# First units of the next batch one place earlier on TensorE, and PSUM tiles shared by the filter stage and the FFN

## The chip, the cores and the metric

The kernel runs on one core of a Trainium2 chip (trn2). The metric is the device time of one execution in microseconds; of several executions the median is taken. All arithmetic is fp32.

## The reference

Two blocks run one after the other. The first is a long convolution of each channel, done by FFT, with a filter that a small MLP makes; the second is a feed-forward network with a maximum of three products.

```python
B, S, D, FO, DFF = 4, 12544, 128, 64, 768
h = (relu(pos_emb @ w1) @ w2) * exp(-0.01 * arange(S))[:, None]   # (S, D)
u = x * v                                                         # (B, S, D)
y = irfft(rfft(u, n=2*S, axis=1) * rfft(h, n=2*S, axis=0), n=2*S)[:, :S]
t = (x * y).reshape(B * S, D)
out = maximum(maximum(t @ W1, t @ W2), t @ W3) @ W_out            # (B*S, D)
```

## The kernel before

The FFT is written as matrix products in three stages, with 90 frequencies k1 in 45 pairs (NK = 45). A batch's input is cut into 32 **units** of four columns. `u_load` brings a unit in, `u_mul` (L375) forms x*v on VectorE, a transpose (`u_turn`, L380) lays it out, and `u_products` (L418) does the first stage: 16 matmuls into one or two PSUM banks, then a copy of half of the result to SBUF on ScalarE (`high`, L440) and two additions per piece on VectorE (L444), which write the tile `spec`. A unit can be done in two halves of 8 matmuls, each with its own bank, copy and pair of additions. The `high` tiles share two buffers.

The program has four parts:

- Up to about 110 us: the filter's MLP, and the first stage of batch 0 and of the filter.
- The **filter stage** (loop at L1101, steps s = 0 to 47). Each step takes one pair of frequencies further: `s_second` and `s_filter` (L1060) make the filter's spectrum, `g_second` the second stage of batch 0, then VectorE multiplies (`g_re`, `g_im`, `g_unfold`, L577 to L589), and three steps later `g_third` (L593) does the inverse stage, whose result ScalarE copies (`zs`, L604) and SP stores in DRAM (`zd`, L605).
- The **passage** out of that loop: steps 45 to 47 have nothing left for `s_second`, and TensorE is given other work between the last three `g_third`: units 0 and 1 of batch 1 (`unit`, L1096), and the folding of the first FFN matrix into the last one. `fold(f)` (L1020) transposes a block of a weight (L1022), ScalarE copies it (`w1t`, L1024), and two matmuls add its product to the tile `pl`; `folding` issues the transpose of f and then the product of f - 1. After that come the units 2, 3 and half of 4 (L1188), the last stage of the first tile (`t_last`, L741), which needs `zd` read back (`zt`, L703) and combined on VectorE (`t_sums`, L734), and the rest of unit 4.
- The **slots**: 32 tiles per batch in six slots each. In a slot TensorE does `up` (two products of the FFN, L156 into `hps`) and `down` (one into `ops`), and beside them steps of the next batch's convolution that `conv_steps` (L608) has laid into slots by hand-written rules. For batch 1, six units are loaded before the slots (`EARLY = 6`), and unit 5's products stand in the third slot (slot number 2, L618). The last batch has no convolution beside it and a shorter form of the second FFN product (`products`).

The order on each engine is the order in which the Python code issues the instructions; an engine takes its instructions in that order, and waits by semaphores. A PSUM tile may be written again only when the readers of its last content are done.

PSUM has eight banks. In the filter stage they are three for `cps` (tag `cv`, taken in turn by `g_second`, `g_third` and `fold`), two for `sps` tag `h` (one tile, `s_filter`), one for `sps` tag `pl` (the turned units, then `pl`), and two for `gps`. The first two units get their banks from a list of their own:

```python
    def banks_of():
        for pool, tag, n in ((gps, "g", 1), (gps, "g", 1), (sps, "h", 2), (gps, "g", 1),
                             (cps, "cv", 1), (gps, "g", 1)):
            yield pool.tile([P, 512 * n], FP32, tag=tag, name="ps1")[:, 0:512]
```

In the slots they are three `hps`, two pairs `cps` (1024 wide) and one `ops`. These pools are opened after the filter stage's are closed.

Of the kernel before, what the change touches and what calls it, by code (L numbers as in the profile page):

```python
# [10 lines left out]
FP32 = mybir.dt.float32  # L11
# [4 lines left out]
PSUM = bass.MemoryType.PSUM  # L16
P = 128
# [25 lines left out]
def tables(NB):  # L43
    S = P * N1
    k1 = np.arange(N1).reshape(2, N1 // 2).T.ravel()
    n = np.arange(NB)
    a = e(np.outer(n, k1 + 0.25) / N1)
    f1 = np.concatenate([a.real, a.imag], 1)
    up = e(np.outer(n + 0.5, k1 + 0.25) / N1)
    f1q = np.stack([np.concatenate([up.real, up.imag], 1), f1], 1)  # L50
    f1h = np.zeros((64 + HH, 2, 2 * N1))
    f1h[:HH, 0], f1h[64:, 0] = f1[:HH], f1[HH:NH]
    f1h[:HH, 1], f1h[64:, 1] = f1[HH:NH], f1[:HH]
    f4 = np.stack([a.T.real, a.T.imag], 1) / S
    f4p = f4[::2].transpose(1, 0, 2).reshape(N1, NB // 2, 2).transpose(0, 2, 1)
    f4 = np.stack([up.T.real, up.T.imag], 1) / S
    f4s = f4[::2].transpose(1, 0, 2).reshape(N1, NB // 2, 2).transpose(0, 2, 1)
    f4q = np.stack([f4p, f4s * np.array([1, -1])[:, None]], 1)
    j, t = np.arange(64), np.arange(64)
    tw = (k1[:, None, None] + 0.25) / S  # L60
    half = []
    for r in range(2):
        s2 = (127 - 2 * t - r)[None, :, None]
        half.append(stacked(e(tw * s2 + j[None, None, :] * s2 / 128)))
    fwd = np.stack(half, 2)
    half = []
    for q in range(2):
        s2 = (2 * t + q)[None, None, :]
        half.append(stacked(e(-tw * s2 - j[None, :, None] * s2 / 128)))
    inv = np.stack(half, 2)  # L70
    both = np.stack([fwd, inv], 2)
    both = both.reshape(N1 // 2, 2, P, 2, 256).transpose(0, 2, 3, 1, 4)
    both = both.reshape(N1 // 2, P, 2, 512)
    j, t = np.arange(32), np.arange(32)
    quarter = [[], []]
    for v in range(2):
        for w in range(2):
            s2 = (63 - 2 * t - v)[None, :, None]
            quarter[0].append(stacked(e(tw * s2 + (2 * j + w)[None, None, :] * s2 / 128)))
            s2 = (2 * t + w)[None, None, :]  # L80
            quarter[1].append(stacked(e(-tw * s2 - (2 * j + v)[None, :, None] * s2 / 128)))
    quarter = np.stack([np.stack(q, 1) for q in quarter], 1)
    quarter = quarter.reshape(N1 // 2, 2, 2, 2, 2, 64, 64).transpose(0, 3, 5, 2, 1, 4, 6)
    quarter = quarter.reshape(N1 // 2, P, 2, 256)
    steps = np.zeros((N1 // 2 + LATE, P, 2, 256))
    steps[:N1 // 2, :, 0], steps[LATE:, :, 1] = quarter[:, :, 0], quarter[:, :, 1]
    f32 = np.float32
    return tuple(np.ascontiguousarray(t, f32) for t in (f1q, f1h, f4q, both, steps))


@with_exitstack
def kernel(
# [289 lines left out]
    def u_turn(u):  # L382
        if u % 2 == 0:
            uts[u] = uts[u + 1] = utp.tile([NB, 16, 2, 32], FP32, tag="uT", name="uT")
        ps = state["turn"]()
        turn(u, ps)
        nc.scalar.copy(uts[u][:, 8 * (u % 2):8 * (u % 2) + 8],
                       ps[0:NB, :].rearrange("n (s t r) -> n s r t", s=8, r=2))
# [62 lines left out]
    def u_first(*args):  # L451
        u_products(*args)()
# [155 lines left out]
    def conv_steps(b, done):  # L608
# [4 lines left out]
        def at(slot, late, fn, *args):  # L613
            out.append((slot, late, len(out), fn, args))

        for u in range(5, done):  # L618
            at(2 * (u - 4), 1, u_first, u)
        lead, low = (1, -NT * NF) if b > 1 else (6, 0)  # L620
        share = UNIT * (NU - done - 1)
        per_pair = (END - lead - 6) / (share + (NK + LATE) // 2 * 2 - 2)
# [147 lines left out]

    def down(i, f, h):
        if f == 0:
            pos_[i] = ops.tile([D, 512], FP32, tag="ops", name="ops")
            halves_mm(pos_[i][:, 0:N], lin[:], gs[i][:].rearrange("d p n -> d (p n)"), True,
                      False)
        halves_mm(pos_[i][:, 0:N], wo_sb[:, f, :], h[:], False, f == NF - 1)
        if f < NF - 1:
            return
        gs.pop(i)
        o = op_.tile([D, 4, NB], FP32, tag="o", name="ot")  # L780
        nc.scalar.copy(o[:].rearrange("d p n -> d (p n)"), pos_.pop(i)[:, 0:N])  # L781
        dst = outT.rearrange("d (p b n) -> d p b n", b=B, n=NB)[:, 4 * i[1]:4 * i[1] + 4, i[0], :]
        nc.gpsimd.dma_start(dst, o[:])  # L783
# [112 lines left out]
    def load_dir(g, a):  # L896
        w = lwp.tile([P, 2, 2, P], FP32, tag=f"w{a}", name="wt")
        nc.sync.dma_start(w[:].rearrange("p k r m -> p (k r m)"), wt_d[g, :, a, :])
        return w
# [100 lines left out]


    cvp = pro.enter_context(tc.tile_pool(name="cvp0", bufs=3))
    cps = pro.enter_context(tc.tile_pool(name="cps0", bufs=3, space=PSUM))
    sps = pro.enter_context(tc.tile_pool(name="sps", bufs=1, space=PSUM))
    gps = pro.enter_context(tc.tile_pool(name="gps", bufs=2, space=PSUM))
    def banks_of():
        for pool, tag, n in ((gps, "g", 1), (gps, "g", 1), (sps, "h", 2), (gps, "g", 1),
                             (cps, "cv", 1), (gps, "g", 1)):
            yield pool.tile([P, 512 * n], FP32, tag=tag, name="ps1")[:, 0:512]

    free = banks_of()

    def bank():
        return next(free)

    state = {"cv": (cvp, cps), "xb": 2, "bank": bank,
             "turn": lambda: sps.tile([P, 512], FP32, tag="pl", name="pst")}
    Gs, minus = {}, {}

    def fold(f):  # L1020
# [72 lines left out]
        if len(folded) > 1:  # L1093
            folded.pop(0)()

    def unit(u):  # L1096
        for h in range(2):
            u_first(u, 2 * h, 2)

    s_minus(0)  # L1100
    for s in range(NK + 3):  # L1101
        if s < NK:
            ws[s, 0] = wf[s]
            s_second(s)
            if s + 1 < NK:
                s_minus(s + 1)
            g_second(s)
            wf.pop(s)
            if s + 3 < NK:
                wf[s + 3] = load_dir(s + 3, 0)  # L1110
        if 1 <= s <= NK:
            g_swap(s - 1)
            s_filter(s - 1)
        if s >= 3:
            ws[s - 3, 1] = wi.pop(s - 3)
            g_third(s - 3)
            if s < NK:
                wi[s] = load_dir(s, 1)
        ready = [g for g in {NK: (s - 2, s - 1)}.get(s, (s - 2,)) if 0 <= g and s <= NK]
        for g in {NK - 2: (s - 2, s - 1), NK - 1: (s - 1,), NK: (s - 1,)}.get(s, (s - 2,)):  # L1120
            if 0 <= g and s <= NK:
                s_store(g)
        for g in ready:
            g_re(g)
            g_im(g)
            g_unfold(g)
        if s < NK:
            g_butterfly(s)

        if s in muls:  # L1130
            u_mul(muls[s])
        if s in turns:
            u_turn(turns[s])
        if s in loads:
            u_load(1, loads[s])
        if s == NK:
            unit(0)
            pl = sps.tile([P, 512], FP32, tag="pl", name="pl")
        if s == NK + 1:
            for f in range(2):  # L1140
                folding(f)
    unit(1)
    state["turn"] = bank
    for f in range(2, NF):
        folding(f)
        if f in (2, 3):
            u_turn(f + 2)
    folded.pop()()
    nc.scalar.copy(lin[:], pl[:, 0:D])
    pro.close()  # L1150
# [11 lines left out]
    wp = conv.enter_context(tc.tile_pool(name="wp", bufs=3))  # L1162
    hh = conv.enter_context(tc.tile_pool(name="hh", bufs=2))
    cvp = conv.enter_context(tc.tile_pool(name="cvp", bufs=3))
    hps = ctx.enter_context(tc.tile_pool(name="hps", bufs=1, space=PSUM))
    cps = conv.enter_context(tc.tile_pool(name="cps", bufs=1, space=PSUM))
    ops = conv.enter_context(tc.tile_pool(name="ops", bufs=1, space=PSUM))
    hbanks = itertools.cycle([hps.tile([P, 512], FP32, name=f"hps{i}") for i in range(3)])
    pairs = itertools.cycle([cps.tile([P, 1024], FP32, name=f"cps{i}") for i in range(2)])
    state = {"bank": lambda: next(pairs)}  # L1170

# [10 lines left out]
    for n, (b, i) in enumerate(tiles[:LAST]):  # L1182
        if i == 0:
            plan, pairs_from = plans[b]
        if n == 0:
            t_load(*tiles[0])
            t_load(*tiles[1])
            second_, third = u_products(2), u_products(3)  # L1188
            fourth = u_products(4, 0, 2, ops.tile([D, 512], FP32, tag="ops", name="ps1"))
            t_sums(tiles[0], nc.vector)  # L1190
            second_()
            fourth[0]()
            t_last(tiles[0], next(hbanks))
            rest = u_products(4, 2, 2, state["bank"]())
            third()
        for f in range(NF):

# [35 lines left out]
    singles = itertools.cycle([cps.tile([P, 512], FP32, name=f"last{i}") for i in range(3)])  # L1233
    state = {"bank": lambda: next(singles)}
    ops = ctx.enter_context(tc.tile_pool(name="ops2", bufs=1, space=PSUM))
    banks = [ops.tile([P, 512], FP32, name=f"ops{i}") for i in range(2)]


    tw = lp.tile([P, 3, NC, 64], FP32, name="tw", bufs=1)
# [12 lines left out]
    for i in range(0, NT, 2):  # L1252
        h = {}
# [67 lines left out]
```

## Time and profile before

| what | value |
|---|---|
| median of 3 runs | 2274.02 us (2273.86 to 2278.21) |
| the profiled execution | 2272.58 us, its span 2270.8 us |
| TensorE busy | 2254.6 us, 99% of the span |
| VectorE / ScalarE / GpSimd busy | 1562.1 / 1175.4 / 879.1 us |
| passage, 281 to 304.3 us | TensorE busy 20.20 of 23.33 us |
| slots of batches 1 to 3, 307.4 to 1850 us | TensorE busy 1541.34 of 1542.59 us |

In the profile, PE is TensorE's matmuls, PEld its weight loads, DVE VectorE, ACT ScalarE, POOL GpSimd and SP the engine that issues most DMAs. An fp32 matmul leaves two records, so that a unit's 16 matmuls show as x32. A bracket after a row gives how long the engine stood idle before it, and what ended that. Lines of the helper `halves_mm` are all L156; the tile names tell them apart (`ps<-ab,wt` is `g_third`, `pl<-wo_sb,w1t` a product of the folding, `hps<-f4p` the last stage, `hps<-gt,w_sb` the FFN).

### The profile page before, as it was taken

The numbers are of one execution on the slowest core, as the hardware profiler recorded it, in microseconds if no ns is written. First come the engines' busy times: TensorE is split into PE (matmuls) and PEld (weight loads), VectorE is DVE, ScalarE is ACT, GpSimd is POOL, SyncE is SP. The second block draws the span as 40 slices with busy tenths as digits, with TensorE's granted clock in tenths as the row PEclk, the third lists the DMA queues.
The fourth block names the chain that finished last, engine by engine and source line by source line (L and its number), as shares of the span: only waits on it lengthen the run. The fifth ranks groups of instructions, "written<-read, shape, count | busy, mean of one in ns | idle before, by whom it ended". The sixth has DMA issues, their size and how long they took to land.

```text
span 2270.8 us, 68490 instructions
## 1 busy us (share of the span) xinstructions
PE 2254.6 (99%) x27855; PEld 1376.4 (61%) x27855; DVE 1562.1 (69%) x2857; ACT 1175.4 (52%) x2130; POOL 879.1 (39%) x1089
## 2 busy tenths in 40 slices
PE   9999999999999999999999999999999999999998
PEld 8999866655555556655555556655555556666665
DVE  5589967677777667667878757667878754444443
ACT  3688844366666534456666534456666522222222
POOL 1145434223333234323333234423333326666666
PEclk9999999999999999999999999999999999999999
DMA  8788999799989589789999789879999732222221
GB/s 194 179 253 277 295 197 182 139 221 248 239 222 244 157 182 178 157 195 252 247 234 231 191 173 178 170 181 244 243 238 236 195 82 56 57 72 65 57 56 22
DMA packets 473365, 411.03 MB, mean 181 GB/s; under 512 B 327993, under 2 KB 374522, under 8 KB 473050
## 3 DMA queue, kind: packets, MB, share of 16 engines
q1 hardware_dynamic: 446034, 329.50, 64.5%
q0 software_dynamic: 26224, 75.44, 11.0%
q8 instruction: 219, 3.59, 0.7%
q10 hardware_dynamic: 792, 1.72, 0.3%
q14 instruction: 96, 0.79, 0.1%
HBM read 262.84 MB, written 84.67 MB: 153 GB/s over the span
## 4 chain that ended last, share of the span: by engine, by line
PE 98%; DVE 1%; DMA 1%; ACT 0%; issue 0%; SPq 0%; POOL 0%; POOLq 0%; DVEq 0%; ACTq 0%
PE hps L156 44%; PE ops L156 19%; PE ops L828 6%; PE cps L428 5%; PE ps L156 4%; PE cps L156 4%; PE cps L495 3%; PE ps L165 3%; PE cps L505 3%; PE sps L1060 2%; PE gps L1042 2%; PE last L156 1%; PE ps L380 1%; PE ps L342 1%; DMA wt<-wt_const 0%; DVE spec L444 0%
## 5 line engine op out<-in xcount | busy, mean ns | idle before, releaser
L156 PE MATMUL hps<-gt,w_sb 128*64 128x392 f32 x6144 | 1149.3, 494 | 0.0
L765 ACT ACTIVATE hid<-hps 128x392 f32<-128x392 f32 x768 | 383.9, 500 | 699.3 <-PE hps L156 679.5
L156 PEld LDWEIGHTS hps<-gt,w_sb 128*64 128x64 f32 x6144 | 431.3, 137 | 420.4 <-issue 384.4
L768 DVE TENSOR_TENSOR hid<-hid,hps 128x392 f32<-128x392 f32 x768 | 428.4, 558 | 331.7 <-PE hps L156 316.2
L156 PE MATMUL ops<-hid,wo_sb 128*64 128x392 f32 x2304 | 480.2, 492 | 0.0
L547 POOL TENSOR_TENSOR cb<-cb,xs 128x512 f32<-128x512 f32 x135 | 174.1, 1290 | 463.6 <-DVE xs L544 346.9
L156 PEld LDWEIGHTS ops<-hid,wo_sb 128*64 128x64 f32 x2304 | 172.3, 137 | 207.0 <-issue 199.4
L520 DVE TENSOR_TENSOR cb<-cps,eo 128x512 f32<-128x512 f32 (+1 forms) x288 | 175.2, 650 | 73.1 <-ACT eo L517 73.1
L444 DVE TENSOR_TENSOR spec<-cps,high 128x360 f32<-128x360 f32 x188 | 140.2, 786 | 118.8 <-ACT high L440 118.7
L783 POOL DMA_DIRECT2D out_dram<-ot x96 | 75.4, 785 | 346.1 <-ACT ot L781 311.6
L535 ACT ACTIVATE xs<-cb 32x512 f32<-32x512 f32 x270 | 169.5, 628 | 20.2 <-DVE cb L520 11.1
L536 ACT COPY xs<-cb 32x512 f32<-32x512 f32 x270 | 166.3, 616 | 3.2
L440 ACT COPY high<-cps 128x360 f32<-128x360 f32 (+1 forms) x94 | 74.8, 796 | 176.8 <-PE cps L428 143.5
L551 DVE TENSOR_TENSOR xs<-cb 128x256 f32<-128x256 f32 x270 | 140.9, 566 | 9.2 <-POOL cb L547 9.0
L428 PEld LDWEIGHTS cps<-f1q,uT 98*64 98x64 f32 x2992 | 129.7, 137 | 28.7 <-issue 23.1
L428 PE MATMUL cps<-f1q,uT 98*64 98x90 f32 x2992 | 134.1, 241 | 2.1 <-DVE uT L411 1.1
L396 POOL COPY planes<-ut 128x784 uint16<-128x784 uint16 x90 | 76.3, 848 | 146.5 <-DVE ut L375 138.1
L528 POOL DMA_DIRECT2D zd<-cb x135 | 92.8, 687 | 61.4 <-DVE cb L520 56.7
L156 PEld LDWEIGHTS cps<-f4p,even 90*64 90x64 f32 x1552 | 89.9, 138 | 34.8 <-issue 32.6
L852 POOL DMA_DIRECT2D out_dram<-o x128 | 77.7, 612 | 51.3 <-DVE o L845 49.1
L156 PE MATMUL cps<-f4p,zt 90*64 90x49 f32 x1552 | 96.3, 222 | 0.0
L156 PE MATMUL cps<-f4p,even 90*64 90x49 f32 x1552 | 95.0, 220 | 0.0
(147 smaller groups left out, 3154.8 us busy)
## 6 DMA issues: line engine op xcount, KB each, us to landing
ht<-hd SPq DMA_DIRECT2D x264, 256.0 KB, 6.8
wt<-wq_const SPq DMA_DIRECT2D x144, 256.0 KB, 6.5
zd<-cb POOLq DMA_DIRECT2D x135, 256.0 KB, 6.1
zt<-zd SPq DMA_DIRECT2D x384, 90.0 KB, 3.0
sq<-spec SPq DMA_DIRECT2D x264, 128.0 KB, 7.0
ut<-in_xr_dram SPq DMA_DIRECT2D x128, 196.0 KB, 3.9
ut<-in_vr_dram SPq DMA_DIRECT2D x128, 196.0 KB, 4.2
xT<-in_x_dram SPq DMA_DIRECT2D x256, 98.0 KB, 3.4
```

The source lines that it names most:

```text
L156: nc.tensor.matmul(out[64 * h:64 * h + 64], lhsT[:, 64 * h:64 * h + 64], rhs, start=start, stop=stop, skip_group_check=True)
L428: nc.tensor.matmul(ps[64 * c:64 * c + 64, 256 * i + h * N1:256 * i + (h + 1) * N1], t[:, 2 * ((at + i) % 8) + h].rearrange("n r t -> n (r ...
L444: nc.vector.tensor_tensor(out=spec[:, :, a, at:at + n], in0=v[:, 1], in1=highs[0], op=op)
L520: nc.vector.tensor_tensor(out=cb[:, a, lo:hi], in0=ps[:, lo:hi], in1=eo[:, lo:hi], op=op)
L528: nc.gpsimd.dma_start(zd[b][2 * z:2 * z + 2].rearrange("k c t a f -> (k c t) a f"), zss.pop(z))
L535: nc.scalar.mul(xs[at:at + 32], xt[at + 32:at + 64], -1.0)
L536: nc.scalar.copy(xs[at + 32:at + 64], xt[at:at + 32])
L547: nc.gpsimd.tensor_tensor(out=xts[g], in0=xts[g], in1=xs[:], op=ALU.add)
L551: nc.vector.tensor_tensor(out=ab[:, q], in0=y[:, 0], in1=y[:, 1], op=(ALU.subtract, ALU.add)[q])
L765: nc.scalar.activation(h[:], pa[:, 0:N], Relu)
L768: nc.vector.tensor_tensor(out=h[:], in0=h[:], in1=pb[:, 0:N], op=ALU.max)
L828: nc.tensor.matmul(ps[64 * c:64 * c + 64, 0:H2], w, rhs[:, H2 * c:H2 * c + H2], start=start, stop=True, skip_group_check=True)
```

## The change

The units move one place up in TensorE's order. Unit 0 (both halves, in the two `gps` banks) is issued ahead of `s_filter(44)` in step 45. Unit 1's first half comes after `g_third(42)`, its second half after the first product of the folding and ahead of `g_third(44)`. Unit 2 is done in halves within the folding. After the folding come the units 3, 4 and the first half of 5, and after the first tile's last stage the second half of 5. Nothing of `u_products` is left in the third slot. ScalarE's copies and VectorE's additions of these pieces keep the order of the units and are issued by `finish`.

PSUM: three tiles `hps` and one tile `solo` are made ahead of the filter stage and kept to the end. `Banks` hands out `hps` in turn where `cps` stood, `up` uses the same three tiles in the slots, `solo` serves the turned units, `pl`, half of unit 5, `ops`, and one of the two tiles of the last batch. Each unit names the bank that it takes: `side()` is one of the two `gps`, `bank()` the next `hps`.

```diff
+class Banks:
+    def __init__(self, tiles):
+        self.tiles = itertools.cycle(tiles)
+
+    def tile(self, shape, dtype, tag, name):
+        return next(self.tiles)
...
-        for u in range(5, done):
-            at(2 * (u - 4), 1, u_first, u)
...
-            pos_[i] = ops.tile([D, 512], FP32, tag="ops", name="ops")
+            pos_[i] = solo
...
-    cps = pro.enter_context(tc.tile_pool(name="cps0", bufs=3, space=PSUM))
+    hps = ctx.enter_context(tc.tile_pool(name="hps", bufs=1, space=PSUM))
+    hps = [hps.tile([P, 512], FP32, name=f"hps{i}") for i in range(3)]
+    solo = ctx.enter_context(tc.tile_pool(name="ops", bufs=1, space=PSUM))
+    solo = solo.tile([P, 512], FP32, name="ops")
     sps = pro.enter_context(tc.tile_pool(name="sps", bufs=1, space=PSUM))
     gps = pro.enter_context(tc.tile_pool(name="gps", bufs=2, space=PSUM))
-    def banks_of():
...
-    free = banks_of()
+    cps = Banks(hps)
 
     def bank():
-        return next(free)
+        return cps.tile([P, 512], FP32, tag="cv", name="ps1")
+
+    def side():
+        return gps.tile([P, 512], FP32, tag="g", name="ps1")
 
     state = {"cv": (cvp, cps), "xb": 2, "bank": bank,
-             "turn": lambda: sps.tile([P, 512], FP32, tag="pl", name="pst")}
+             "turn": lambda: solo}
...
-    def unit(u):
-        for h in range(2):
-            u_first(u, 2 * h, 2)
+    def finish(parts):
+        for fn in parts:
+            fn()
...
+        if s == NK:
+            unit0 = [u_products(0, 2 * h, 2, side()) for h in range(2)]
         if 1 <= s <= NK:
             g_swap(s - 1)
             s_filter(s - 1)
...
         if s == NK:
-            unit(0)
-            pl = sps.tile([P, 512], FP32, tag="pl", name="pl")
+            for part in unit0:
+                finish(part)
+            part = u_products(1, 0, 2, bank())
+            pl = solo
         if s == NK + 1:
+            finish(part)
             for f in range(2):
                 folding(f)
-    unit(1)
+            part = u_products(1, 2, 2, side())
+    finish(part)
     state["turn"] = bank
+    part = u_products(2, 0, 2, side())
+    both_ = sps.tile([P, 1024], FP32, tag="h", name="ps1")
     for f in range(2, NF):
         folding(f)
         if f in (2, 3):
             u_turn(f + 2)
+        if f == 3:
+            finish(part)
+            part = u_products(2, 2, 2, both_)
+    finish(part)
     folded.pop()()
     nc.scalar.copy(lin[:], pl[:, 0:D])
     pro.close()
...
-    hps = ctx.enter_context(tc.tile_pool(name="hps", bufs=1, space=PSUM))
     cps = conv.enter_context(tc.tile_pool(name="cps", bufs=1, space=PSUM))
-    ops = conv.enter_context(tc.tile_pool(name="ops", bufs=1, space=PSUM))
-    hbanks = itertools.cycle([hps.tile([P, 512], FP32, name=f"hps{i}") for i in range(3)])
+    hbanks = itertools.cycle(hps)
...
-            second_, third = u_products(2), u_products(3)
-            fourth = u_products(4, 0, 2, ops.tile([D, 512], FP32, tag="ops", name="ps1"))
+            second_, third = u_products(3), u_products(4)
+            fourth = u_products(5, 0, 2, solo)
             t_sums(tiles[0], nc.vector)
             second_()
             fourth[0]()
             t_last(tiles[0], next(hbanks))
-            rest = u_products(4, 2, 2, state["bank"]())
+            rest = u_products(5, 2, 2, state["bank"]())
             third()
...
-    banks = [ops.tile([P, 512], FP32, name=f"ops{i}") for i in range(2)]
+    banks = [solo, ops.tile([P, 512], FP32, name="ops1")]
```

More of the change, by code (lines that the diff above doesn't have):

```diff
@@ L1002 @@
     cvp = pro.enter_context(tc.tile_pool(name="cvp0", bufs=3))
-    cps = pro.enter_context(tc.tile_pool(name="cps0", bufs=3, space=PSUM))
+    hps = ctx.enter_context(tc.tile_pool(name="hps", bufs=1, space=PSUM))
+    hps = [hps.tile([P, 512], FP32, name=f"hps{i}") for i in range(3)]
+    solo = ctx.enter_context(tc.tile_pool(name="ops", bufs=1, space=PSUM))
+    solo = solo.tile([P, 512], FP32, name="ops")
     sps = pro.enter_context(tc.tile_pool(name="sps", bufs=1, space=PSUM))
     gps = pro.enter_context(tc.tile_pool(name="gps", bufs=2, space=PSUM))
-    def banks_of():
-        for pool, tag, n in ((gps, "g", 1), (gps, "g", 1), (sps, "h", 2), (gps, "g", 1),
-                             (cps, "cv", 1), (gps, "g", 1)):
-            yield pool.tile([P, 512 * n], FP32, tag=tag, name="ps1")[:, 0:512]
-    free = banks_of()
+    cps = Banks(hps)
     def bank():
-        return next(free)
+        return cps.tile([P, 512], FP32, tag="cv", name="ps1")
+    def side():
+        return gps.tile([P, 512], FP32, tag="g", name="ps1")
     state = {"cv": (cvp, cps), "xb": 2, "bank": bank,
-             "turn": lambda: sps.tile([P, 512], FP32, tag="pl", name="pst")}
+             "turn": lambda: solo}
     Gs, minus = {}, {}
```

## The prediction

> **What bounds the kernel now.** I read the page first: busy times, then the chain that ended last.
>
> ```profile
> span 2270.8 us, 68490 instructions
> PE 2254.6 (99%) x27855; PEld 1376.4 (61%) x27855; DVE 1562.1 (69%) x2857; ACT 1175.4 (52%) x2130; POOL 879.1 (39%) x1089
> ...
> PE 98%; DVE 1%; DMA 1%; ACT 0%; issue 0%; SPq 0%; POOL 0%; POOLq 0%; DVEq 0%; ACTq 0%
> ```
>
> TensorE works 2254.6 of 2270.8 us, and the change removes none of its matmuls. So the change can win only idle time of TensorE, or lose by making some. Where that idle lies is read from the stretches: span, PE, PEld, DVE, ACT, POOL busy (with counts), clock, DMA share, GB/s.
>
> ```profile
> 281.00:304.33 23.33, 20.20 (x335) 15.60 (x335) 15.31 (x33) 12.98 (x29) 4.88 (x7) 1.00 0.64 177
> ...
> 307.41:1850.00 1542.59, 1541.34 (x17581) 856.11 (x17578) 1126.98 (x1997) 850.65 (x1535) 509.43 (x600) 1.00 0.90 204
> ```
>
> The whole passage, 281 to 304.3 us, has 23.33 - 20.20 = 3.13 us of idle; the 1542 us of convolution after it have 1.25. Even a passage without any idle gives 3.13 us, 0.14% of the time. The timeline of TensorE shows each gap in brackets, with what ended it:
>
> ```profile
> 281.83 1.10 PE L1060 MATMUL sps<-w2x,G 64*64 64x128 f32 x32 [0.79 <-ACT ht L1076]
> 282.86 1.09 PE L156 MATMUL ps<-ab,wt 128*64 128x128 f32 x16
> 283.79 1.41 PE L428 MATMUL ps<-f1q,uT 98*64 98x90 f32 x32
> 285.67 1.09 PE L156 MATMUL ps<-ab,wt 128*64 128x128 f32 x16 [0.47 <-DMA wt<-wt_const]
> 286.69 0.44 PE L1022 MATMUL pt<-eye,w_sb 128*128 128x128 f32 x2
> 287.61 0.44 PE L156 MATMUL pl<-wo_sb,w1t 128*64 128x128 f32 x4 [0.47 <-ACT w1t L1024]
> 287.98 1.09 PE L156 MATMUL ps<-ab,wt 128*64 128x128 f32 x16
> 288.87 1.44 PE L428 MATMUL ps<-f1q,uT 98*64 98x90 f32 x32
> ...
> 298.51 0.32 PE L156 MATMUL hps<-f4p,zt 90*64 90x49 f32 x4 [0.40 <-DVE zt L734]
> ```
>
> Here 283.79 is unit 0, 288.87 unit 1, and the three L156 rows `ps<-ab,wt` are the last `g_third`. Against them stand VectorE and ScalarE:
>
> ```profile
> 286.73 0.76 DVE L589 TENSOR_TENSOR ab<-xt 128x256 f32<-128x256 f32 x2
> 287.41 0.56 DVE L375 TENSOR_TENSOR ut<-ut 128x392 f32<-128x392 f32 x1
> 287.88 1.10 DVE L444 TENSOR_TENSOR spec<-ps,high 128x180 f32<-128x180 f32 x4
> 290.29 1.23 DVE L444 TENSOR_TENSOR spec<-ps,high 128x180 f32<-128x180 f32 x4 [1.30 <-ACT high L440]
> ```
>
> The DVE rows have no bracket until 290.29: VectorE runs without a pause up to 288.98, and unit 0's additions (L444) end only then, though its matmuls ended at 285.2. That lag decides this case.
>
> **What the skill says.** PSUM — Partial Sum Buffer, section "Engine vs sequencer instructions": the queues of ScalarE and VectorE are strict FIFO, and matmuls start and complete in program order. The trace agrees: ACT's `w1t` copy at 287.28 stands behind `zs` at 286.80, and PE's next product behind both. Same page, "PSUM bank collisions raise a hardware error": a bank must be guarded until its reader is done; the 0.79 gap above is such a wait (one `sps` tile, read by ACT L1076). TensorE: Matmul & The Clock Gate, "What's actually happening": after an idle window of about 3.4 us the array falls to half clock. Here the clock column is 1.00 in the passage and falls only after the last matmul, which ends at 2263.26:
>
> ```profile
> 2265.50:2266.00 0.50, 0.00 (x0) 0.00 (x0) 0.00 (x0) 0.00 (x0) 0.50 (x2) 0.92 0.51 100
> 2266.00:2271.00 5.00, 0.00 (x0) 0.00 (x0) 0.00 (x0) 0.00 (x0) 0.36 (x1) 0.50 0.10 20
> ```
>
> 0.92 over half a microsecond is 0.08 of 0.5 at half clock, so it fell at about 2265.9: 2.7 us of idle sufficed, less than the page's window.
>
> **The change, part by part.** A unit is 16 matmuls, 32 records; 64 records from 294.52 to 297.05 give 1.27, and 32 from 306.17 in the chain 1.24 with its ends cut; I take 1.33 us (41.6 ns a record). Nothing moved issues a DMA; SP and POOL keep their orders.
>
> 1. Unit 0 goes ahead of `s_filter(44)`. It needs nothing late, and covers the 0.79 wait for ht. `s_filter(44)` then ends near 283.5; ACT, busy until 283.55 with L572, copies it at 283.6 as before (283.57). Gain 0.79, no loss.
> 2. The first half of unit 1 (0.67) goes ahead of `g_third(43)`. TensorE gets there at 285.1, and the weights still land at 285.54 (a DMA of 6.60 us issued at 278.94): `g_third(43)` starts at 285.67 as before.
> 3. Here the new wait appears. The banks now go round three: `g_third(42)`, half of unit 1, `g_third(43)`, fold 0, **fold 1**. So fold 1 writes the bank of unit 1's first half, and needs VectorE's additions on it. They come in VectorE's order after unit 0's: the first half of unit 0 is through at 288.47 (287.88 + 0.59 for two). Only then is its `high` buffer free (two buffers), so ACT's `high` for unit 1 runs 288.5 to 289.0 (0.48), VectorE adds 289.05 to 289.65 (0.60), and fold 1 starts at 289.76 (0.11 from such an end to a weight load, as 299.92 to 300.03 shows). Before, fold 1 started at 286.8. Loss about 2.95, in place of the 0.47 for w1t. Queued behind it on TensorE: the first product into `pl`, the second half of unit 1, and `g_third(44)`.
> 4. `g_third(44)` thus starts at 289.76 + 0.11 + 0.33 + 0.67 = 290.87 instead of 287.96: 2.9 later. On it hangs the chain of the page: zs, zd stored (2.37 us), zt loaded, `even` at 297.05, the last stage at 298.51, the first FFN product at 300.70. All shift by 2.9. Meanwhile TensorE has as much filler as before: unit 1, 2, 3 and half of 4 became unit 2, 3, 4 and half of 5. Unit 3 now waits for VectorE on unit 2's second half (near 297.05, some 0.8 after the last fold), and the filler ends at 300.4, beneath `even` at 300.0 + 0.6: no further cost.
> 5. Unit 5 leaves the third slot (305.97): 1.33 less there, with full gain since TensorE has no gap there. ACT and DVE save 0.80 and 1.50 in the slots, off the path: nothing.
> 6. Halving unit 2 and 5 and making 4 whole adds two additions on VectorE and a copy on ACT, about 0.3 each, beside the wait of the chain: nothing. The bank numbers (one bank for turns, `pl` and `ops`; pairs one bank up; the tail's ops0 the old `ops`) give the same order and the same releasers two uses back: nothing; if that cover failed, a wait would show at the first pair, some tenths.
>
> Sum: +2.9 - 1.33 = +1.6 us, from 0 (a shorter wait, next part) to +2.9 (the saving eaten, second rival). The profiled execution took 2272.58 (span 2270.8 and 1.8 around it), so 2274.2; the median of the runs shown is 2274.02, 1.4 above it. I put the change on the median: 2275.6.
>
> **The unknown costs.** The wait in step 3 doesn't exist before. Below: if only ACT's read held the bank and the `high` buffer were free, w1t would still queue behind `high`: zs to 287.39, high to 287.9, w1t to 288.15, a gap of about 1.3, so g_third 1.3 later and in sum 0. Above: DVE's pair at 0.75 instead of 0.60 and ACT late by 0.3: 3.5 and in sum +2.1. I take 2.95, since every term has a row. I exclude a gain above 3.13.
>
> **Rivals.**
> - *The waits just go* (the two first gaps closed, fold 1 not held): -0.79 and half a unit's cover, up to -1.3: 2272.7. For it: both gaps are real. Against: VectorE's unbroken row to 288.98.
> - *The loads come late too.* SP's loads for unit 6 stand behind zt and shift by 2.9, TensorE in the slots only by 1.6. Unit 6 is joined until 316.98 and used at 318.05: 1.07 slack against 1.3. Then up to 1.3 comes back: +2.9, 2276.9. It decides if the join is bound by DMA; but ACT's L411 at 315.37 follows an activation without a bracket.
> - *Slower: the clock gate.* A gap of 2.9 us at 287 to 289.8 behind one of 0.6 at 285 is as long as the 2.7 that the end of the trace shows to be enough. At half clock from 289.8 for the 4.8 us that the start shows (first matmul at 1.19, six records a microsecond in the stretch from 3 to 5, twelve from 6 on), half is lost: 2.4; +1.6 + 2.4 = +4.0, 2278.0, up to 2279. It decides when the gap exceeds about 2.7 us and the window falls right. Against: the window's phase is unknown, and 1.0 us of matmuls lie in between.
>
> **How the numbers follow.** A measurement of this kernel tells 0.2%, 4.5 us, from no change. Forecast (+0.8 to +2.2) 0.60; waits just go 0.13; late loads 0.10; clock gate 0.17, of which less than half passes 4.5. Faster by over 0.2% is beyond the idle there is: 0.02 for a surprise. Slower: 0.08 from the gate and the unknown. Same: 0.90. Range 2272.4 to 2278.8: from the first rival to the gate's upper part.
>
> **What would show it.** Right: a gap of 2.5 to 3 us ahead of one L1022 transpose, released by DVE spec; no gap before L1060; `g_third(44)` near 290.9; `even` near 300; L428 gone from the third slot. Wrong: that gap under 1 us; a clock column under 1.00 in the passage; new brackets on TensorE's rows after 310; any change of 4 us.

## The result: 3.4 us slower, and the profile after

| | before | after |
|---|---|---|
| median, 22 runs each | 2275.33 us (2273.13 to 2278.28) | 2278.77 us (2277.43 to 2281.25) |
| ratio, 95% interval | | 1.0016, [1.001, 1.0022] |
| the profiled execution (span) | 2272.58 us (2270.8) | 2277.88 us (2276.1) |

The kernel is slower by 0.1 to 0.22%. Lines of after are 7 or 8 higher than those of before: `halves_mm` is L164, `u_products` L436 and L452, `fold` L1029 and L1031, `s_filter` L1067. The page of after:

```profile
span 2276.1 us, 68491 instructions
PE 2255.9 (99%) x27855; PEld 1377.0 (60%) x27855; DVE 1562.2 (69%) x2859; ACT 1175.7 (52%) x2131; POOL 878.9 (39%) x1089
...
PE 97%; DVE 1%; issue 0%; ACT 0%; DMA 0%; SPq 0%; POOL 0%; POOLq 0%; DVEq 0%; ACTq 0%
```

The same 27855 matmul records take 1.3 us more, and the span has 20.2 us of TensorE idle where it had 16.2. Part of that arises ahead of the change: `g_third(41)`, the last third stage ahead of the passage, starts at 279.95 us in the profile before, at 281.53 in this one, at 280.88 in a repeat of the changed kernel, and between 280.2 and 282.1 in the profiles of the other experiments, though all these kernels issue the same work up to there. (Before is the earliest of the 14 profiles, so these starts alone do not rule out that the new tiles cost a few tenths there.) So I compare times **from the start of g_third(41)**; "after" at t is put beside "before" at t - 1.58. The timeline of TensorE after, the rows that answer to those shown of before:

```profile
281.53 1.09 PE L164 MATMUL hps<-ab,wt 128*64 128x128 f32 x16
282.45 1.41 PE L436 MATMUL ps<-f1q,uT 98*64 98x90 f32 x32
283.79 1.10 PE L1067 MATMUL sps<-w2x,G 64*64 64x128 f32 x32
...
285.75 0.79 PE L436 MATMUL hps<-f1q,uT 98*64 98x90 f32 x16
286.88 1.09 PE L164 MATMUL hps<-ab,wt 128*64 128x128 f32 x16 [0.34 <-DVE xt L585]
287.91 0.33 PE L1029 MATMUL hps<-eye,w_sb 128*128 128x128 f32 x1
291.38 0.30 PE L1029 MATMUL hps<-eye,w_sb 128*128 128x128 f32 x1 [3.14 <-DVE spec L452]
291.61 0.69 PE L164 MATMUL ops<-wo_sb,w1t 128*64 128x128 f32 x4
292.09 1.42 PE L436 MATMUL ps<-f1q,uT 98*64 98x90 f32 x16
293.29 1.87 PE L164 MATMUL hps<-ab,wt 128*64 128x128 f32 x16
```

The wait for ht ahead of `s_filter(44)` (0.79 before) is gone: unit 0 runs straight into L1067. A single wait of 3.14 us now stands ahead of fold 1's transpose (L1029, `hps`). What the prediction's sum did not have is in the second column of the last three rows: half a unit takes 1.42 us instead of 0.79, and `g_third(44)` 1.87 instead of 1.09. The stretches of after (span, PE, PEld, DVE, ACT, POOL busy, clock, DMA share, GB/s) point to a cause; the clock is the share of full TensorE clock that was granted:

```profile
288.16:291.57 3.41, 0.27 (x2) 0.14 (x1) 2.88 (x10) 1.02 (x3) 0.00 (x0) 1.00 0.72 235
291.57:294.98 3.41, 3.41 (x37) 3.37 (x38) 0.00 (x0) 0.27 (x1) 0.00 (x0) 0.50 0.02 5
294.98:298.40 3.42, 3.42 (x48) 2.50 (x46) 0.60 (x2) 2.27 (x6) 0.00 (x0) 1.00 0.33 97
```

The clock column, the one before DMA share, falls to 0.50 as the gap ends and stays there for 3.41 us. Before, it was 1.00 through the whole passage. The rows of VectorE and ScalarE show that the gap itself is the one that was predicted (VectorE first, then ScalarE):

```profile
289.46 1.09 DVE L452 TENSOR_TENSOR spec<-ps,high 128x180 f32<-128x180 f32 x4
290.64 0.60 DVE L452 TENSOR_TENSOR spec<-hps,high 128x180 f32<-128x180 f32 x2
```

```profile
290.14 0.47 ACT L448 COPY high<-hps 128x180 f32<-128x180 f32 x1 [1.53 <-DVE spec L452]
290.41 0.30 ACT L1031 COPY w1t<-hps 128x128 f32<-128x128 f32 x1
```

VectorE gets to unit 0 at 289.46, ScalarE's `high` for unit 1 waits 1.53 us for the buffer, VectorE adds from 290.64, and fold 1 starts at 291.38. Behind `high` in ScalarE's order stands `w1t` of fold 0.

Along the passage the delay against before, from the start of `g_third(41)`, is: `g_third(44)` starts 3.73 later (11.76 against 8.03) and ends 4.5 later; the first FFN product starts 4.75 later (300.70 - 279.95 = 20.75 before, 307.03 - 281.53 = 25.50 after). Its rows, before and after:

```profile
300.70 4.15 PE L156 MATMUL hps<-gt,w_sb 128*64 128x392 f32 x24
```

```profile
307.03 4.17 PE L164 MATMUL hps<-gt,w_sb 128*64 128x392 f32 x24 [0.30 <-DVE gt L761]
```

After the third slot, now without unit 5, the delay is 3.56 (33.72 against 30.16, the product after the last stage of the second tile), and 3.76 one product further, where `hid` of VectorE is late. From there on nothing is gained or lost: the 3.8 us of the profile stand beside the 3.4 of the medians.

### The profile page after: what moved, and what is told of

It is laid out like the page before. It is cut to its first block, busy times and chain, and to the rows that moved or that the text cites. A ratio compares the mean times of both kernels' runs of the same rounds, so it can differ in the third digit from the quotient of the medians.

```text
span 2276.1 us, 68491 instructions
## 1 busy us (share of the span) xinstructions
PE 2255.9 (99%) x27855; PEld 1377.0 (60%) x27855; DVE 1562.2 (69%) x2859; ACT 1175.7 (52%) x2131; POOL 878.9 (39%) x1089
## 3 DMA queue, kind: packets, MB, share of 16 engines
q10 hardware_dynamic: 792, 1.72, 0.3%
## 4 chain that ended last, share of the span: by engine, by line
PE 97%; DVE 1%; issue 0%; ACT 0%; DMA 0%; SPq 0%; POOL 0%; POOLq 0%; DVEq 0%; ACTq 0%
PE hps L164 48%; PE ops L164 19%; PE ops L834 6%; PE cps L436 5%; PE cps L164 4%; PE cps L503 3%; PE ps L173 3%; PE cps L513 3%; PE sps L1067 2%; PE gps L1049 2%; PE last L164 1%; PE ps L388 1%; PE ps L350 1%; PE ps L164 1%; DVE spec L452 0%
## 5 line engine op out<-in xcount | busy, mean ns | idle before, releaser
L164 PE MATMUL hps<-gt,w_sb 128*64 128x392 f32 x6144 | 1149.2, 494 | 0.3 <-DVE gt L761 0.3
L164 PEld LDWEIGHTS hps<-gt,w_sb 128*64 128x64 f32 x6144 | 430.6, 137 | 422.2 <-issue 391.6
L164 PE MATMUL ops<-hid,wo_sb 128*64 128x392 f32 x2304 | 480.1, 492 | 0.0
L164 PEld LDWEIGHTS ops<-hid,wo_sb 128*64 128x64 f32 x2304 | 172.0, 137 | 207.2 <-issue 203.6
L452 DVE TENSOR_TENSOR spec<-cps,high 128x360 f32<-128x360 f32 x186 | 138.7, 786 | 118.3 <-ACT high L448 118.3
L436 PEld LDWEIGHTS cps<-f1q,uT 98*64 98x64 f32 x2960 | 128.4, 137 | 28.7 <-issue 24.4
L436 PE MATMUL cps<-f1q,uT 98*64 98x90 f32 x2960 | 132.7, 241 | 2.6 <-DVE uT L419 1.5
L164 PEld LDWEIGHTS cps<-f4p,even 90*64 90x64 f32 x1552 | 89.7, 138 | 34.9 <-issue 33.6
L164 PE MATMUL cps<-f4p,zt 90*64 90x49 f32 x1552 | 96.3, 222 | 0.0
L164 PE MATMUL cps<-f4p,even 90*64 90x49 f32 x1552 | 95.0, 220 | 0.0
```

Source lines behind the costliest of these rows:

```text
L164: nc.tensor.matmul(out[64 * h:64 * h + 64], lhsT[:, 64 * h:64 * h + 64], rhs, start=start, stop=stop, skip_group_check=True)
L436: nc.tensor.matmul(ps[64 * c:64 * c + 64, 256 * i + h * N1:256 * i + (h + 1) * N1], t[:, 2 * ((at + i) % 8) + h].rearrange("n r t -> n (r ...
L452: nc.vector.tensor_tensor(out=spec[:, :, a, at:at + n], in0=v[:, 1], in1=highs[0], op=op)
```

## The experiments

**Is it the clock?** Theory: the later chain costs the predicted 1.6 us and the clock about 1.7 more. Rivals: the clock costs nothing, or the shared tiles do. Filler matmuls into an unused half of `solo` keep TensorE busy in the gap and change no wait; seven pairs, and three.

```diff
-            for f in range(2):
-                folding(f)
+            folding(0)
+            for _ in range(7):    # e5_fill3: range(3)
+                halves_mm(solo[:, 256:512], eye[:], w_sb[1][:, 0:256], True, True)
+            folding(1)
```

> The changed kernel with seven pairs of 128x256 matmuls put on TensorE between fold 0 and fold 1, into a part of the folding's bank that nothing reads (about 3.0 us at full clock). Every wait of the changed kernel stays: fold 1 still waits for VectorE's additions. Theory A (the clock gate: the wait of 3.14 us empties a window of activity, and 3.4 us at half clock follow): the clock column stays 1.00 through the passage, g_third(44) takes 1.09 us instead of 1.87, and the kernel is about 2 us faster than the changed one, +1.2 to +2.0 us on the kernel before. Theory B (the wait alone sets the loss, the clock is a bystander): no difference from the changed kernel, +3.4 us on before.

Measured: 2276.35 us against 2274.24 for the kernel before (medians), ratio 1.0012, [1.0004, 1.002]. The timeline of TensorE:

```profile
286.86 3.24 PE L164 MATMUL ops<-w_sb,eye 128*64 128x256 f32 x28
290.05 0.31 PE L1029 MATMUL hps<-eye,w_sb 128*128 128x128 f32 x1
290.29 0.44 PE L164 MATMUL ops<-wo_sb,w1t 128*64 128x128 f32 x4
290.56 0.79 PE L436 MATMUL ps<-f1q,uT 98*64 98x90 f32 x16
291.18 1.04 PE L164 MATMUL hps<-ab,wt 128*64 128x128 f32 x16
```

Fold 1 starts as late as before the filling (290.05 - 280.17 = 9.88 after `g_third(41)`, against 9.85), but `g_third(44)` takes 1.04 us and half a unit 0.79: the clock is 1.00. The first FFN product comes 23.78 us after `g_third(41)` instead of 25.50, 1.72 us earlier. In this profile useless work made the kernel faster. The medians of the two kernels come from different sets of runs, so they were run once more side by side:

> The changed kernel as it is, beside its filled twin on the same chip. Theory (1.6 us from the later chain less the saved unit, and 1.7 us from one clock window of 3.41 us at half speed): +3.3 us against the kernel before, a mean clock of 0.998 or less in four of five runs. Rival (the clock costs nothing, the whole is the chain): +3.3 us too, but the filled twin the same.

> The changed kernel with seven pairs of 128x256 matmuls in its gap, beside the unfilled one. Theory (the clock costs 1.7 us): +1.6 to +2.1 us against the kernel before and 1.2 to 1.7 us less than the unfilled one; mean clock 0.999 in at least three of four runs. Rival (the clock costs nothing): the same time as the unfilled one, +3.3 us.

Measured: the changed kernel 2279.29, ratio 1.0021, [1.0013, 1.0029]; with the filler 2276.28, 1.001, [1.0001, 1.0018]; the kernel before 2274.02. Of the 13 runs with the filler 11 are faster than every one of the 14 without.

How often did the clock fall? A run without a profile gives only its mean clock. One stretch of 3.41 us at half clock takes 3.41 / 2 / 2274 = 0.00075 off that mean. In the 14 profiles the mean is 0.9988 to 0.9994 where the clock held until the last matmul, and 0.9976 to 0.9984 where it fell in or just behind the passage; so I count a mean of 0.998 or less as a fall, knowing that the count is rough. It is 13 of 14 runs without the filler, 1 of 13 with it, and 3 of 42 of the kernel before in this set.

The difference is 2.5 us by the ratios, 3.0 by the medians, more than the 1.7 expected. The profiles show two ways to more. The first is two stretches at half clock in this run of the changed kernel:

```profile
286.98:290.39 3.41, 0.17 (x1) 0.00 (x0) 3.22 (x10) 1.11 (x3) 0.00 (x0) 1.00 0.80 254
290.39:293.81 3.42, 3.08 (x31) 2.88 (x33) 0.20 (x1) 0.27 (x1) 0.00 (x0) 0.50 0.07 24
293.81:297.22 3.41, 3.41 (x33) 2.65 (x30) 0.60 (x2) 1.23 (x3) 0.00 (x0) 0.50 0.29 83
```

The gap ended a little after 290.39, so the window that followed began with 0.34 us of idle, and the clock came back only after the next, which was full. The first FFN product is then 25.90 us after `g_third(41)`, against 23.83 in the filled twin: 2.07. The second is a wait in the slots: one FFN product waits 1.01 us (<-DVE hid) here and 0.29 in the filled twin, 0.7 us more that are not matmuls at half clock; what `hid` waits for is shown below.

> The changed kernel with three pairs of 128x256 matmuls (0.463 us a pair, as measured with seven) into a free half of `solo` between the transposes of fold 0 and fold 1; they cover 1.39 us of the 3.14 us gap. Theory (a gap must come near to one clock window of 3.4 us): what is left, 1.75 us, does not drop the clock; clock 1.00 through the passage, about 2276.4, +2.1 us against the kernel before, as with the seven pairs. Rival (the share of idle time in a window counts): half a window idle still drops it in a part of the runs; between +2.1 and +3.4 us. Rival (the clock is not what costs; shared tiles or late loads are): +3.4 us as without filler.

Measured: 2277.43, ratio 1.0014, [1.0005, 1.0022], which tells neither from +2.1 nor from +3.4. In its profile a gap of 1.81 us was left and the clock stayed at 1.00; the window that holds most of it:

```profile
286.64:290.06 3.42, 1.90 (x17) 0.91 (x13) 3.23 (x10) 1.16 (x3) 0.00 (x0) 1.00 0.81 259
```

By the mean clock it fell in 6 of 13 runs, against 4 of 26 with the seven pairs, but also in 13 of 49 of the kernel before in the same set, which has no such gap. So these runs do not settle whether 1.8 us of idle lowers the clock; the next experiment shows a fall behind a gap of 2.41 us, well short of a whole window.

**What makes the wait?** One edit: another bank for unit 1's first half.

```diff
-            part = u_products(1, 0, 2, bank())
+            part = u_products(1, 0, 2, sps.tile([P, 1024], FP32, tag="h", name="ps1"))
```

> The changed kernel with one edit: unit 1's first half goes to the `sps` tile h instead of the `hps` tile that fold 1 writes two uses later. Theory (two causes end at nearly the same time): fold 1 no longer waits, but ScalarE's copy w1t of fold 0 still stands behind `high` of that half, which waits for a `high` buffer until 1.53 us later; the first product into `pl` then waits some 2.6 us, the whole is 0.4 us better than the changed kernel, and the clock still falls: about +3 us against the kernel before. Rival (the bank alone makes the wait): a gap of 0.5 to 0.8 us, no fall of the clock, about 0 to +0.5 us.

Measured: 2276.74 against 2274.34, ratio 1.0007, [0.9999, 1.0015]. Fold 1 no longer waits, and the product behind it does:

```profile
288.24 0.44 PE L1029 MATMUL hps<-eye,w_sb 128*128 128x128 f32 x2
291.08 0.44 PE L164 MATMUL ops<-wo_sb,w1t 128*64 128x128 f32 x4 [2.41 <-ACT w1t L1031]
...
291.98 1.74 PE L164 MATMUL hps<-ab,wt 128*64 128x128 f32 x16
```

The bank was one of two causes that end close together; ScalarE's order is the other. The clock fell here too: TensorE was busy 1.08 us of the 3.41 ahead of the fall, and `g_third(44)` took 1.74. By the mean clock it fell in 7 of 13 runs. Both causes go when the finishing of that half is issued behind the two foldings as well:

```diff
-            finish(part)
             for f in range(2):
                 folding(f)
+            finish(part)
             part = u_products(1, 2, 2, side())    # e2_nowait
```

> The changed kernel with unit 1's first half in the two-bank tile of s_filter instead of one of the three hps, and its copy and additions issued after both w1t copies. Fold 1 then waits for nothing of unit 1, and w1t for no high. Theory A (bank plus ScalarE's order made the wait, the wait made the half clock): no gap over 0.7 us between g_third(43) and g_third(44), clock 1.00, g_third(44) about 1.3 us later than before, saved again in the third slot: -0.5 to +0.3 us on before. Theory C (moving the units itself costs, by late loads or by the new bank places): still +1.5 or more.

The next one also moves the second half of unit 1 out of the loop, behind `g_third(44)`:

```diff
-            part = u_products(1, 2, 2, side())
+    part = u_products(1, 2, 2, side())        # e3_third_first, after the loop
```

> As the kernel without the wait, and unit 1's second half behind g_third(44) instead of ahead of it. Theory A: g_third(44) starts when it did before (about 7.1 us after the start of g_third(41) plus half a unit hidden), the store and reload of zd shift by 0, the last stage by 0.0 to 0.4 us since there is half a unit more between, and the third slot gives back 1.33: -1.3 to -0.7 us on before. If slower than before, the gain in the third slot doesn't exist or something later in the slots is late.

Measured: 2274.39, ratio 1.0004, [0.9995, 1.0012], and 2275.07, 1.0003, [0.9995, 1.0011]: neither can be told from before, although a unit has left the third slot. By the medians the first is at +0.2 us, within its forecast; the second was forecast at -1.3 to -0.7 and is at +0.8. In the first, no wait ahead of `g_third(44)` was to be over 0.7 us, and one is 0.82: from L1067 to the first FFN product they are 0.35, 0.48, 0.82, 0.66, 0.51 and 0.33, together 3.15 us; before, the six of the passage were 0.79, 0.47, 0.47, 0.36, 0.40 and 0.53, 3.02 us. The idle time only found other places. In the second, the FFN product behind the last stage of the second tile comes 28.84 us after `g_third(41)`, 1.32 earlier than before (30.16), but two products further it is 33.67 against 34.15: 0.84 is lost again. VectorE's timeline there:

```profile
312.55 0.57 DVE L383 TENSOR_TENSOR ut<-ut 128x392 f32<-128x392 f32 x1 [0.81 <-DMA ut<-in_vr_dram]
313.03 0.56 DVE L774 TENSOR_TENSOR hid<-hid,hps 128x392 f32<-128x392 f32 x1
```

`hid` stands behind a `u_mul` (L383) whose load is late, and TensorE waits for it (0.62 <-DVE hid). The same order stands behind the 1.01 us in the repeat of the changed kernel: `u_mul` there waits 0.87 us for its load, and `hid` follows it. By the mean clock, the clock also fell in 5 of the 13 runs of the second kernel (2 of 13 of the first, 8 of 41 of the kernel before in that set). One edit puts that `u_mul` one slot later, and one more adds a filler pair in two waits:

```diff
-            mul = max(load_ + 2, int(s) - 6)
+            mul = max(load_ + (3 if b == 1 else 2), int(s) - 6)    # e11_late_mul
...
+            halves_mm(solo[:, 256:512], eye[:], w_sb[1][:, 0:256], True, True)    # e12, after folding(0)
...
+            halves_mm(solo[:, 256:512], eye[:], w_sb[1][:, 0:256], True, True)    # e12, ahead of unit 3
```

> The version with unit 1's first half in the `sps` tile and its second half behind g_third(44), and one more edit: `u_mul` of the first units in the slots one slot later, behind `hid` on VectorE. Theory (in that version VectorE's `hid` stands behind a `u_mul` whose loads come late, since SP's loads follow zt and the slots begin one unit earlier; TensorE waits 0.62 us and some tenths for it): those waits go, 0.8 us less than that version, -0.5 us against the kernel before (between -1.4 and +0.4). Rival (the loads are late for the join too, so the wait only moves): a new wait ahead of unit 6's products, +0.3 us against the kernel before.

> The version with `u_mul` one slot later, and one pair of 128x256 matmuls (0.46 us) each into `solo` in two of its waits: that for w1t of fold 0 and that ahead of unit 3. Theory (short waits within a clock window add up, so that a part of the runs loses 1.7 us to the clock): mean clock below 0.999 in no more than 1 run of 10, 0.3 us less than the version without the pairs. Rival (waits under 1 us do not touch the clock): the same time and the same clocks as without the pairs.

Measured: 2274.63, ratio 0.9999, [0.9991, 1.0007], and 2274.54, 1.0, [0.9992, 1.0008]. In the profile of the first the wait for `hid` shrank to 0.36 us, one product further on, and at that product the kernel stood 0.47 us better than without the edit (33.20 against 33.67) and 0.95 better than before (34.15). The times cannot show that: -0.5 us was forecast for it, and the medians have +0.6, the ratio none. The clock fell in 2 of 13 and 1 of 13 runs; whether short waits lower it, this does not decide. No version here beats the kernel before by what these runs can tell.

**Is the saved unit worth its 1.33 us?** Unit 5 goes back to the third slot.

```diff
+        for u in range(5, done):
+            at(2 * (u - 4), 1, u_first, u)
...
-            second_, third = u_products(3), u_products(4)
-            fourth = u_products(5, 0, 2, solo)
+            second_ = u_products(3)
+            fourth = u_products(4, 0, 2, solo)
...
-            rest = u_products(5, 2, 2, state["bank"]())
-            third()
+            rest = u_products(4, 2, 2, state["bank"]())
```

> The changed kernel with unit 5 put back into the third slot, and the filler of the passage one unit shorter (units 3 and 4, as half of 4 took half of 5's place). Theory (the chain from g_third(44) to the first FFN product sets the passage, so that filler is free there and a unit in the slot costs its 1.33 us): first FFN product at the same time after the last fold, 1.33 us more in the third slot; +4.7 us against the kernel before. Rival (filler sets the passage): no difference, +3.4 us.

Measured: 2278.93 against 2274.34, ratio 1.002, [1.0014, 1.0027]: between the two runs of the changed kernel (1.0016 and 1.0021), so the times do not decide. The profile says more. It has two stretches at half clock, so it is put beside the repeat of the changed kernel, which has them too; `g_third(44)` starts 11.92 us after `g_third(41)` here and 11.91 there. The first FFN product comes at 25.37 here and 25.90 there, and the unit's row in the slot takes 1.41 us, 1.24 from start to start. So the unit does cost 1.24 us in the slot, but in this pair its place ahead of the first FFN product was not free either: it cost 0.53, and moving it saved 0.7 us. Without it the product waited for VectorE's `gt` (0.80); in the repeat it waited for nothing, as TensorE was still at the filler, part of which had run at half clock.

**Do the shared tiles cost?** The old order with the new tiles (e4_tiles), and then the same with small matmuls in the waits around the first tile's last stage (e8_old_order_filled, whose additions are shown).

```diff
+            last = next(hbanks)
+            halves_mm(last[:, 392:512], eye[:], w_sb[1][:, 0:120], True, True)
+            beside(last)          # two such pairs
-            t_last(tiles[0], next(hbanks))
+            t_last(tiles[0], last)     # and beside(ps) after its first product
+            beside(hps[(hps.index(last) + 1) % 3])
```

> The order of the kernel before on every engine, with the PSUM tiles of the changed one (three hps and one solo kept from the filter stage to the end). All theories but C: no difference, within 0.3 us in the profile's stretches from 281 us to the end. Theory C: a part of the +3.4 us here.

> The order before the change with the tiles of after it, as in the run that took +2.3 us, and small matmuls (128x120, 0.22 us a pair) in the three waits around the first last stage: three pairs ahead of it, two after its first product, two behind it. Theory (that run was slow since its clock fell around the last stage, and the tiles themselves cost nothing): clock 1.00 there in nearly all runs, 2274.3, 0 us against the kernel before (within 0.8). Rival (the shared tiles themselves cost): +1.5 to +2.3 us, at a clock of 1.00. Rival (the clock falls elsewhere): a mean clock of 0.998 or less in half of the runs, and +1 to +2 us.

Measured: 2276.53, ratio 1.001, [1.0002, 1.0019], and 2275.3, 1.0001, [0.9992, 1.0009]. The first was a surprise. Its timeline has nearly the rows of before, but its clock fell right behind the last stage, and the first FFN product took 5.43 us instead of 4.15:

```profile
297.38:300.79 3.41, 2.09 (x52) 1.69 (x49) 2.83 (x4) 1.00 (x2) 0.00 (x0) 1.00 0.58 130
300.79:304.20 3.41, 3.41 (x24) 2.06 (x22) 1.94 (x3) 1.11 (x3) 2.00 (x2) 0.50 0.66 184
```

By the mean clock it fell in 9 of 13 runs, and with the filler in 1 of 13. So, once the clock is held up, the tiles themselves cost nothing that can be measured. In the window ahead of the fall TensorE waits three times, 0.40, 0.40 and 0.52 us, between short matmuls; the kernel before has such waits too, and its clock fell in 24 of 132 runs in these three sets. Why it falls more often with the new tiles was not found.

## Why the prediction was wrong

Forecast was +1.6 us with +0.8 to +2.2 as its own range; measured were +3.4 and, in the repeat, +5.3 (medians). 2278.77 lies at the very end of the range that was given, 2272.4 to 2278.8, and only since the clock rival was in it. All these times stood on a median of three runs of before, 2274.02. On that of the 22 runs, 2275.33, the same forecast would be 2276.9 and the clock rival 2279.3, so that the measured time lies nearer to the rival.

1. *Unit 0 ahead of `s_filter(44)`*: right, the gap of 0.79 us is gone.
2. *Half a unit ahead of `g_third(43)`*: right, and a little better: it starts 0.37 us earlier than forecast, held by VectorE's xt rather than the weights.
3. *The new wait*: right to the tenth. Fold 1 was forecast at 289.76 and starts at 291.38 - 1.58 = 289.80, for the reasons given. The lower bound (a gap of 1.3) supposed both the bank and a `high` buffer free; with the bank alone freed the gap is still 2.41 us, since `high` waits for its buffer.
4. *`g_third(44)` and its chain 2.9 later*: **the step that failed.** It took the matmuls behind the gap at full clock, and gave the clock gate 0.17 as a rival. It should have been the forecast. The start is 291.71 instead of 290.87 on the scale of before, and `g_third(44)` lasts 1.87 us, so that its end, where the chain starts, is 4.5 us late and not 2.9. The rival's price of 2.4 us on the whole was near: 1.72 and 2.07 by the two pairs of profiles; the 2.5 by the ratios has the longer wait for `hid` in it. It took 4.8 us at half clock; the profiles have 3.41 or 6.83. Its trigger was argued badly. The prediction took from the end of the trace that 2.7 us of idle suffice; the fall there lies on the same grid of 3.41 us, behind a window in which TensorE was busy 0.75 us. "The window's phase is unknown" was counted for the forecast, but a gap of 3.1 to 3.6 us takes at least 1.5 us out of some window of 3.41 wherever the windows lie, and more than half of one in most positions: 50 of the 57 runs with that gap (the changed kernel's 36, 21 with unit 5 back) had a mean clock of 0.998 or less.
5. *Unit 5 out of the third slot, -1.33*: right in kind, a little too large: 1.19 by the profile (4.75 before the slot, 3.56 after it), 1.24 by unit 5 put back. The prediction's own rows gave 1.27 and 1.24. That the filler ahead costs nothing (step 4) did not hold where the clock was at half for two windows: 0.53.
6. *Banks and halves, nothing*: right for the banks, by the last pair of experiments; the halving of units was not tested alone.

Of the second rival (late loads) the mechanism was real, but it acts at `u_mul` ahead of `hid` on VectorE, not at the join: 0.2 us in after, 1.01 in the repeat of the changed kernel, 0.62 and 0.96 in two of the experiments. It is the second reason why the repeat is slower than the forecast. With the clock held up by the filler the kernel is at +2.1 and +2.3 us: the forecast's +1.6 and the few tenths of this wait. The 3.8 us of the profile come out as 2.9 for the wait, 1.6 for the clock up to the end of `g_third(44)`, 0.25 at the first FFN product, which waits for `gt` besides, less 1.2 for the unit, and 0.2 for `hid`.

## What to carry to other kernels

A new wait on TensorE costs its length and a chance of 3.41 or 6.83 us at half clock behind it, which fall on the very matmuls that the wait made late: here in 50 of 57 runs with a gap of 3.1 to 3.6 us and in 7 of 13 with one of 2.41. Price it in the forecast, not as an accident. Before moving work ahead of a wait, write down for each bank it takes who reads it, what that reader has queued ahead, and who takes the bank next; here three orders (TensorE's, ScalarE's, VectorE's) closed the gap at the old place and opened a larger one. A run with useless matmuls in the gap separates the wait from the clock in one step.

## What the runs showed of the hardware

- The stretches between two changes of the clock, as the traces record them, are multiples of 3.413 us in all 14 traces: in after 286.72 (84 times), 3.41 (once) and 1976.32 (579 times), in the first profile with seven pairs 2263.04 (663 times), in the repeat of the changed kernel 6.83 at half clock (twice). So within a run the clock changes on one grid. Its phase differs from run to run: the first rise comes 4.1 to 7.2 us after the start. The Trainium skill, TensorE: Matmul & The Clock Gate, section "What's actually happening", gives a free-running window of 3413 ns; the traces agree.
- The same section has the clock fall after an idle window. Here a window did not have to be idle throughout: the clock fell behind windows with TensorE busy 0.17 us (the repeat), 0.27 (after), 0.84 (unit 5 back), 1.08 (another bank) and even 2.09 of 3.41 (old order, new tiles: 52 records, 32 of them of the short matmuls of the last stage), and it stayed up behind one with 1.90 (three pairs). So busy time in the profile alone does not give the threshold; it is left open.
- In or behind the passage it rose again, in all five traces in which it had fallen, only behind a window with TensorE busy throughout; windows with 3.08 (the repeat) and 2.81 us (unit 5 back) busy at half clock were not enough. At the start of the program, though, one with 2.92 of 3.41 us was enough (the second profile with seven pairs, first matmul at 1.19, rise at 4.11). So what it takes to rise is left open too.
